# Reordering two short VectorE chains in a fused linear-attention and two-layer kernel

## The chip, the cores and the metric

The kernel runs on one core of one Trainium2 chip. The metric is device time in microseconds (us), as the median of several executions. Besides the time there is a trace of one execution per kernel, taken by the hardware profiler, with the start and length of each instruction on TensorE (PE, and PEld for its weight loads), VectorE (DVE), ScalarE (ACT), GpSimd (POOL) and the DMA queues.

## The reference

Eight batches of linear attention, then two dense layers on the result:

```python
q_p, k_p = phi(q), phi(k)                  # phi(x) = (x if x > 0 else exp(x) - 1) + 1
kv  = einsum('bhsd,bhse->bhde', k_p, v)
z   = sum(k_p, axis=2)
num = einsum('bhsd,bhde->bhse', q_p, kv)
den = einsum('bhsd,bhd->bhs', q_p, z)[..., None] + 1e-06
x   = (num / den) reshaped to [4608, 512]
h   = x @ w_in                             # 512 -> 2048
out = (h - tanh(h)) @ w_out                # 2048 -> 512
```

q, k and v are [8, 8, 576, 64]. Inputs and output are float32.

## The kernel before

The 4608 rows are worked in nine blocks of 512. A block has a first layer (16 tiles of four matmuls, `l1mm`), then a second layer in 16 "slots" of four matmuls (`l2mm`). The attention of the batch that the next block needs is put between these, as functions appended to a slot (`s2[n]`, run after the matmuls of slot n). The batch 0 attention comes first, in an opening that has no dense work to hide behind. In the code, `z` is the sum of k, `kv` the product of k and v, `zc` and `kz` their masked copies out of PSUM on VectorE, `den` the denominators, `split` the reciprocal cut into bf16 pieces (its last result is called w), and `spread` the matmuls that broadcast w to where the numerators stand.

The opening, where the first change acts:

```python
    b0_zc(0)            # VectorE: z of the first pairs out of PSUM
    b0_kv(0)            # TensorE: kv of the first pairs
    b0_kz(0)            # VectorE: kv of the first pairs out of PSUM
    b0_z(1)             # TensorE: z of the second pairs
    b0_zc(1)            # VectorE: z of the second pairs out of PSUM
    a_den(0, Banks([4]))   # TensorE: den; its second half needs zc(1). Then 1/den on VectorE
    ns0 = new_ns(0)
    b0_rest()
    b0_num(0, ns0)      # TensorE: num; needs kz(0)
    b0_kv(1)
    b0_kz(1)
    b0_spread((0, 2), 0)   # TensorE: needs 1/den
```

The second layer of the first block, where batch 1 is prepared (cut):

```python
            s2[3].append(lambda: a_qphi(1, 0))
            s2[4].append(lambda: (a_qphi(1, 1), load_q(2), load_k(2), load_v(2)))
            s2[0].append(prepare)
            s2[7].append(lambda: (a_qT_pe(1, 0, side), a_kv(1, side), a_qT_pe(1, 1, side)))
            s2[8].append(lambda: b0_scale_rest(side))
            s2[9].append(lambda: (a_den(1, side), num1(), a_split(1)))
            s2[11].append(lambda: spread1(0))
            # ... cut: exp2 = an exponential of batch 2 on ScalarE, rest2 = its VectorE part
            s2[11].append(lambda: (exp2(qs, q_t, qp_t, "qp", 0), rest2(qs[0])))
            s2[12].append(lambda: exp2(qs, q_t, qp_t, "qp", 1))
            s2[13].append(lambda: (spread1(1), exp2(ks, k_t, kp_t, "kp", 0), rest2(qs[1]), a_qT_dma(2)))
            s2[14].append(lambda: rest2(ks[0]))
```

The output copies of this block (`evac`, on ScalarE) come after slots 12 to 15.

## Time and profile before

| | before |
|---|---|
| median of 3 executions | 293.37 us (293.27 to 293.65) |
| span in the trace | 291.8 us |
| TensorE busy | 285.5 us, 98% |
| VectorE busy | 175.1 us, 60% |
| ScalarE busy | 139.7 us, 48% |

TensorE is full by this table, but its busy time counts modelled lengths: a dense 128x512 matmul is drawn 0.379 us long and the next one starts 0.216 us after it, so a wait of up to 0.16 us between two of them does not show in it, and a longer one shows only in part. Such a wait shows as a late start: one that comes later than 0.216 after the start before it, or than that plus 0.095 where the tile size changes.

### The profile page before, as it was taken

Reading aid. Unit: us, or ns where it says so; the run is one execution under the profiler, and the core shown is the slowest. Engines: PE = TensorE matmul, PEld = TensorE weight load, DVE = VectorE, ACT = ScalarE, POOL = GpSimd, SP = SyncE. Lnnn points to the kernel's source line nnn. Section 1 sums busy time; section 2 is a strip of 40 time slices with the busy share of each in tenths; the row PEclk is TensorE's granted clock in tenths of the full one; section 3 lists DMA queues with packets and bytes.
Section 4 is the critical chain, followed back from the end, with each engine's and each line's share of the span. In section 5 each row is a group of like instructions: output and inputs, shape, how many; then the busy total and the mean of one; then the engine's idle time right before and its main releaser. Section 6 shows DMA issues by size and latency. Waiting matters only on the chain.

```text
span 291.8 us, 4505 instructions
## 1 busy us (share of the span) xinstructions
PE 285.5 (98%) x1803; PEld 134.5 (46%) x1803; DVE 175.1 (60%) x266; ACT 139.7 (48%) x168; POOL 33.7 (12%) x56
## 2 busy tenths in 40 slices
PE   8999999999999999999999999999999999999994
PEld 3544464454454444444454444444544444444443
DVE  4759958987468674776478637865581457106600
ACT  4938548846354733465345534751551155126411
POOL 8674030110030003000300030000000000000000
PEclk9999999999999999999999999999999999999999
DMA  7999999997999768965895579666117310130032
GB/s 105 193 202 212 208 206 215 194 183 149 249 158 161 175 128 137 197 146 121 136 223 123 123 139 197 146 138 139 30 38 165 73 36 0 43 83 19 0 74 72
DMA packets 39093, 38.94 MB, mean 133 GB/s; under 512 B 16352, under 2 KB 33824, under 8 KB 38304
## 3 DMA queue, kind: packets, MB, share of 16 engines
q0 software_dynamic: 17568, 18.35, 39.0%
q1 hardware_dynamic: 21344, 20.17, 30.9%
q8 instruction: 14, 0.23, 0.3%
q10 hardware_dynamic: 160, 0.13, 0.1%
q14 instruction: 7, 0.06, 0.1%
HBM read 43.91 MB, written 9.55 MB: 183 GB/s over the span
## 4 chain that ended last, share of the span: by engine, by line
PE 85%; DMA 11%; POOL 2%; issue 1%; DVE 0%; POOLq 0%
PE ps_all L387 39%; PE ps_all L366 38%; DMA v<-in_v_dram 6%; DMA w_in_sb<-in_moe_w_in_dram 3%; PE ps_all L199 2%; DMA kraw<-in_k_dram 2%; PE ps_all L317 2%; PE ps_all L618 1%; PE ps_all L276 1%; POOL v L419 1%; PE ps_all L177 1%; POOL qraw L90 0%; PE ps_all L320 0%; POOL qraw L93 0%; POOL w_out_sb L115 0%
## 5 line engine op out<-in xcount | busy, mean ns | idle before, releaser
L366 PE MATMUL ps_all<-xT,w_in_sb 128*128 128x512 bf16 x574 | 127.6, 379 | 0.0
L387 PE MATMUL ps_all<-w_out_sb,gT 128*128 128x512 bf16 x560 | 127.5, 379 | 0.0
L373 DVE TENSOR_TENSOR gT<-ps_all,th 128x1024 bf16<-128x1024 f32 x64 | 77.9, 1218 | 59.2 <-ACT th L372 59.2
L372 ACT ACTIVATE th<-ps_all 128x1024 f32<-128x1024 f32 x64 | 65.6, 1025 | 57.1 <-PE ps_all L366 46.5
L366 PEld LDWEIGHTS <-w_in_sb 128*128 128x128 bf16 x574 | 55.0, 98 | 66.1 <-issue 0.3
L387 PEld LDWEIGHTS <-gT 128*128 128x128 bf16 x560 | 54.2, 98 | 64.2
L396 ACT COPY osb<-ps_all 128x512 f32<-128x512 f32 (+1 forms) x36 | 20.9, 583 | 71.8 <-PE ps_all L387 52.6
L328 DVE TENSOR_TENSOR xT<-ps_all,rdb 128x512 bf16<-128x512 f32 x24 | 16.5, 691 | 13.7 <-PE ps_all L317 11.2
L134 ACT ACTIVATE e<-qraw 128x1152 bf16<-128x1152 bf16 x16 | 18.5, 1160 | 8.2 <-DMA qraw<-in_q_dram 8.2
L134 ACT ACTIVATE e<-kraw 128x1152 bf16<-128x1152 bf16 x15 | 17.5, 1164 | 0.3 <-DMA kraw<-in_k_dram 0.3
L136 DVE TENSOR_TENSOR qp<-e,r 128x1152 bf16<-128x1152 bf16 x16 | 12.1, 758 | 8.0 <-ACT e L134 7.2
L136 DVE TENSOR_TENSOR kp<-e,r 128x1152 bf16<-128x1152 bf16 x15 | 11.4, 759 | 7.9 <-ACT e L134 6.9
L383 POOL COPY g<-qT 1x1 bf16<-1x1 bf16 x5 | 0.9, 178 | 119.2 <-DMA qT<-qp 119.2
L378 DVE TENSOR_TENSOR gT<-ps_all,th 128x512 bf16<-128x512 f32 x16 | 10.3, 686 | 2.4 <-ACT th L377 1.7
L377 ACT ACTIVATE th<-ps_all 128x512 f32<-128x512 f32 x16 | 9.2, 598 | 4.4 <-PE ps_all L366 3.2
L447 PE MATMUL ps_all<-zero 128*128 128x512 bf16 x29 | 9.2, 480 | 1.2 <-DVE zero L405 1.2
L317 PE MATMUL ps_all<-qT,kz 128*128 128x512 bf16 x28 | 10.1, 379 | 0.0
L135 DVE TENSOR_SCALAR r<-qraw 128x1152 bf16<-128x1152 bf16 x16 | 7.3, 454 | 2.1 <-DMA qraw<-in_q_dram 2.1
L199 PEld LDWEIGHTS <-kp 64*128 64x128 bf16 x216 | 6.4, 94 | 2.5 <-issue 2.1
L285 DVE RECIPROCAL rden<-den 128x144 f32<-128x144 f32 x7 | 7.4, 1053 | 0.2
L199 PE MATMUL ps_all<-vp,kp 64*128 64x136 bf16 x216 | 7.4, 220 | 0.0
L394 DVE COPY osb<-ps_all 128x128 f32<-128x128 f32 x1 | 0.3, 292 | 11.6 <-PE ps_all L618 11.6
(85 smaller groups left out, 123.6 us busy)
## 6 DMA issues: line engine op xcount, KB each, us to landing
out_dram<-osb SPq DMA_DIRECT2D x70, 128.0 KB
rdb<-ds SPq DMA_DIRECT2D x12, 576.0 KB
kraw<-in_k_dram POOLq DMA_DIRECT2D x7, 576.0 KB, 7.1
qraw<-in_q_dram POOLq DMA_DIRECT2D x7, 576.0 KB, 9.1
v<-in_v_dram POOLq DMA_DIRECT2D x7, 576.0 KB, 11.6
w_in_sb<-in_moe_w_in_dram POOLq DMA_DIRECT2D x6, 256.0 KB, 8.7
w_out_sb<-in_moe_w_out_dram POOLq DMA_DIRECT2D x3, 512.0 KB, 14.7
qraw<-in_q_dram POOLq DMA_DIRECT2D x2, 288.0 KB, 4.4
```

The lines of the kernel that those rows point to most:

```text
L134: return (lambda: nc.scalar.activation(e, x, AF.Exp), lambda: nc.vector.tensor_scalar(r, x, 0.0, 1.0, ALU.max, ALU.add), lambda: nc.vector ...
L136: lambda: nc.vector.tensor_tensor(y, e, r, ALU.min))
L199: nc.tensor.matmul(ps[hg][:, i, :], kp[r, i, j].rearrange("p h d -> p (h d)"), vp[r, i, j, :], start=(j == 0), stop=(j == J - 1))
L317: nc.tensor.matmul(ps, kz[:, p // 2, p % 2, 0:128], qT[:, p % 2, 0:8, p // 2, :], start=True, stop=True)
L328: nc.vector.tensor_mul(xT[:, p, S * b:S * b + 512].rearrange("p (j t c) -> p j t c", j=8, t=4), ps.rearrange("p j (t c) -> p j t c", t=4), ...
L366: nc.tensor.matmul(h, w_in_sb[:, 2 * (p % 2) + p // 2, fi * 128:(fi + 1) * 128], xT[:, p, c * 512:(c + 1) * 512], start=(n == 0), stop=(n ...
L372: nc.scalar.activation(th, h, AF.Tanh)
L373: nc.vector.tensor_sub(gT[:, fi:fi + 2, :], h, th)
L377: nc.scalar.activation(th, h, AF.Tanh)
L378: nc.vector.tensor_sub(gT[:, fi, :], h, th)
L387: nc.tensor.matmul(o, gT[:, fi, i * 128:(i + 1) * 128], w_out_sb[:, fi, :], start=(fi == 0), stop=(fi == NF - 1))
L396: nc.scalar.copy(osb[:, f0:f1], o[:, f0:f1])
```

## The change

The intent is to shorten two dependent chains. In the opening (the first part of the diff, below the "opening hunk"), den's second half waits for the z copy, which stands behind a kv copy on VectorE's queue; z is put first. In batch 1 (the "slot hunks"), den, num and split are run one slot sooner, and the two spreads with them.

```diff
     b0_zc(0)
     b0_kv(0)
-    b0_kz(0)
     b0_z(1)
     b0_zc(1)
+    b0_kz(0)
     a_den(0, Banks([4]))
...
-            s2[8].append(lambda: b0_scale_rest(side))
-            s2[9].append(lambda: (a_den(1, side), num1(), a_split(1)))
-            s2[11].append(lambda: spread1(0))
+            s2[8].append(lambda: (b0_scale_rest(side), a_den(1, side), num1(), a_split(1)))
+            s2[10].append(lambda: spread1(0))
...
-            s2[11].append(lambda: (exp2(qs, q_t, qp_t, "qp", 0), rest2(qs[0])))
-            s2[12].append(lambda: exp2(qs, q_t, qp_t, "qp", 1))
-            s2[13].append(lambda: (spread1(1), exp2(ks, k_t, kp_t, "kp", 0), rest2(qs[1]), a_qT_dma(2)))
+            s2[11].append(lambda: exp2(qs, q_t, qp_t, "qp", 0))
+            s2[12].append(lambda: (spread1(1), exp2(qs, q_t, qp_t, "qp", 1), rest2(qs[0])))
+            s2[13].append(lambda: (exp2(ks, k_t, kp_t, "kp", 0), rest2(qs[1]), a_qT_dma(2)))
```

## The prediction

> **What bounds the kernel now.** I read the page's busy shares first, then TensorE's own waits.
>
> ```profile
> PE 285.5 (98%) x1803; PEld 134.5 (46%) x1803; DVE 175.1 (60%) x266; ACT 139.7 (48%) x168; POOL 33.7 (12%) x56
> ```
>
> ```profile
> engine line waited for: us in total, times, longest us
> PE ps_all L447 <- DVE zero L405: 1.2, 1, 1.2
> PE ps_all L221 <- DMA v<-in_v_dram: 0.5, 1, 0.5
> PE ps_all L177 <- DMA v<-in_v_dram: 0.2, 1, 0.2
> PE ps_all L240 <- DVE xT L244: 0.2, 1, 0.2
> ```
>
> TensorE is the bound: busy for 98% of 291.8 us, with 2.1 us of listed waits, 1.2 of them before its first instruction. The change acts in two stages alone, the opening (to 18 us) and batch 1 (37 to 52 us), so I took the timeline there, by start times and not by lengths: a 128x512 matmul shows 379 ns but a new one starts every 216 ns, so a short wait hides inside the records. In the opening (VectorE and TensorE lines of the timeline, 8 to 20 us; start, length, engine, line):
>
> ```profile
> 12.37 0.40 PE L210 MATMUL ps_all<-one,kp 64*128 64x32 bf16 x18
> 12.59 0.43 DVE L225 TENSOR_TENSOR kz<-ps_all,mask 128x256 bf16<-128x256 f32 x1 [0.24 <-PE ps_all L221]
> 12.93 0.21 DVE L214 TENSOR_TENSOR kz<-ps_all,mask 128x64 bf16<-128x64 f32 x1
> 13.20 0.12 PEld L276 LDWEIGHTS <-kz 128*32 128x32 bf16 x8 [0.32 <-DVE kz L214]
> 13.44 0.61 PE L231 MATMUL ps_all<-qT,kz 128*128 128x512 bf16 x2
> 13.56 1.06 DVE L285 RECIPROCAL rden<-ps_all 128x144 f32<-128x144 f32 x1 [0.41 <-PE ps_all L276]
> 14.76 0.73 PE L240 MATMUL ps_all<-rden,sel 32*128 32x128 f32 x16
> ```
>
> The second half of the den matmuls (L276) stands 0.3 us behind the z copy (L214), which stands behind the kv copy (L225). That is the wait the first hunk aims at. Next I looked at what follows: two lines of the chain that ended last, then the timeline from 36 us.
>
> ```profile
> 22.32 16.50 DMA v<-in_v_dram
> 38.87 1.66 PE ps_all L177 x36
> ```
>
> ```profile
> 37.16 0.76 DVE L136 TENSOR_TENSOR qp<-e,r 128x1152 bf16<-128x1152 bf16 x1 [0.74 <-ACT e L134]
> 37.97 0.51 PEld L164 LDWEIGHTS <-qp 128*128 128x128 bf16 x9 [0.32 <-DVE qp L136]
> 38.87 1.43 PEld L177 LDWEIGHTS <-kp 64*128 64x128 bf16 x36 [0.40 <-DMA v<-in_v_dram]
> 45.77 0.37 DVE L298 SCALAR_TENSOR_TENSOR w<-t,part,u 128x144 bf16<-128x144 bf16 x1
> 46.20 0.30 PE L354 MATMUL ps_all<-w,sel 32*128 32x144 bf16 x8
> 47.34 1.16 ACT L134 ACTIVATE e<-qraw 128x1152 bf16<-128x1152 bf16 x1 [1.40 <-DMA qraw<-in_q_dram]
> 50.24 8.07 PE L366 MATMUL ps_all<-xT,w_in_sb 128*128 128x512 bf16 x36
> 51.47 1.07 ACT L396 COPY osb<-ps_all 128x512 f32<-128x512 f32 x2
> 52.10 5.71 PEld L366 LDWEIGHTS <-w_in_sb 128*128 128x128 bf16 x27 [0.26 <-issue]
> ```
>
> Three gates stand here, in order: v of batch 1 lands just before 38.87; the split reciprocal w ends at 46.14; the third output copy ends near 52.05 and the ninth matmul of the next block (PSUM bank 2) starts at 52.10. Before 38.87 the chain that ended last runs through DMA and GpSimd, not TensorE. After 52.10 TensorE starts its dense matmuls at an even 216 ns, apart from a switch of about 0.095 wherever it goes to smaller tiles (50.24 + 36 x 0.216 + the wait of 0.13 below = 58.15, and the next group, of 64-row tiles, starts at 58.24) or back.
>
> **What the Trainium skill says.** "Perfetto Trace Analysis", section "Tensor Engine Instruction (MATMUL, LD_WEIGHTS)", says a matmul's end is estimated from its size and not observed. The trace agrees: lengths of 379 ns at a pitch of 216; hence I count by starts. "PSUM — Partial Sum Buffer", section "Engine vs sequencer instructions", says ScalarE's and VectorE's queues are strictly first in, first out. The trace agrees: the z copy stood behind the kv copy although its matmuls' modelled end was 12.77 (12.37 + 0.40), and the output copies stand behind the exponentials. The same page, "PSUM bank collisions raise a hardware error", says to guard PSUM by bank and quadrant; here the bank-2 matmul starts at 52.10, 0.05 after the copy that empties that bank.
>
> **The change, part by part.** No instruction is added or removed; comparing the instruction orders, TensorE has four L387 matmuls moved from before the den group to behind the second spread, VectorE has z and kv swapped in the opening and the second pair of scalings moved ahead of the first q piece of batch 2; on ScalarE and the DMA queues the order is the same.
>
> Opening. Three latencies come from the lines: matmul end to copy start 0.04 (kv: end 12.55, copy 12.59), copy end to weight load 0.06 (13.14 to 13.20), and a VectorE successor starting 0.09 before its predecessor's end (12.93 against 13.02). With z first: z copy at 12.77 + 0.04 = 12.81 instead of 12.93, end 13.02, den resumes at 13.08 instead of 13.20: 0.12 sooner. The kv copy moves back: start 12.93, end 13.36. The num matmuls (L231) need it: 13.36 + 0.06 = 13.42 against 13.44, so TensorE gains only 0.02 there; den alone would have let them start at 13.32, and 0.10 of the 0.12 turns into a wait for kv. The reciprocal starts at 13.44 and ends at 14.50 instead of 14.62. If the spread (L240) waited for it, the gain is 0.12; if it waited for TensorE's own queue (its matmuls carry "issue" as cause), 0.02. So the opening is 0.02 to 0.12 us shorter up to the first dense matmul at 17.68.
>
> It does not get through. The transposes at 37.98 start right when qp is there (37.92 + 0.06), which hangs on a q load; and nine transposes take 0.52 us to the next start (40.46 to 40.98 for the later nine), so TensorE could start L177 at about 38.59 (37.98 + 0.52 + the switch of 0.095) and waits until 38.87 for v: 0.28 us. An earlier TensorE only waits longer. Net: 0.00.
>
> Batch 1. Before, den runs at 42.91 after the four matmuls of slot 9; after, at once behind the rest of batch 0: 4 x 0.216 = 0.865 sooner, 42.05. Its inputs are there (kz ends at 41.45, the last qT copy at 41.79). Bank reuse holds: num's third matmul needs the batch 0 rest product (ends 42.58) and comes at 42.75; the next needs den's copy (ends about 42.84) and comes at 42.97. So den, reciprocal and split all come 0.865 sooner, w at 45.27 instead of 46.14. But spread is moved by one slot as well. Between num and spread there are eight L387 matmuls before and eight after, so TensorE reaches the spread 0.865 sooner too: now 44.27 + 8 x 0.216 = 46.00, plus the 0.095 switch, 46.09, against w's 46.14 + 0.06. The real wait of 0.10 is kept, at 45.3. The second spread keeps its two slots behind the first as well. TensorE's work is the same, so the next block begins at 50.24 again. What really comes sooner is the last product for xT: the four scalings run together and end near 49.2 to 49.8 instead of 50.62. Its first reader is the fourth matmul of the block, at 50.24 + 3 x 0.216 = 50.89; 50.62 + 0.06 was in time already, so this buys slack of a microsecond and no time. Net: 0.00.
>
> Third gate. From 47.34 ScalarE runs without a gap: exp, copy, exp, copy, exp, copy, and starts when the q load lands. Its order is the same in both kernels. TensorE is ready for bank 2 at 50.24 + 8 x 0.216 = 51.97 and waits 0.13. Whatever batch 1 gained would be lost here too. Sum: 0.00 + 0.00, with the noise of where the loads land.
>
> **The rivals.** (1) The opening's gain gets through: 293.37 - 0.12 = 293.25. For: a TensorE at 98% passes on what it gains. Against: the v wait in the list. (2) The chain den to w is what counts, so all three gates fall: 0.28 + 0.10 + 0.13 = 0.51, 292.86. Against: the v and q loads do not start later or sooner with this change; over the first 60 us the software DMA queue took 98.6% of sixteen engines' time, so they land when the bytes are through. (3) Worse: VectorE now holds back the q pieces of batch 2 behind the second pair of scalings (the min of the first piece by about 1 us), and with it the transpose DMA of batch 2, the gate of the next loads at 56.88. Against: the last piece hangs on the exponential that ends at 50.03, and VectorE is then free; it should end near 51.6 instead of 51.85. If it did cost: 293.6 to 293.9.
>
> **Range and chances.** I take 293.3, with a little for the opening in runs where v lands sooner. Runs of before differ by 0.38 (293.27 to 293.65), by my reading where loads land, so 292.95 to 293.65. Two per cent is 5.9 us, more than ten times everything in rival 2: faster 0.005, slower 0.01, same 0.985.
>
> **What would show it.** Right: z's copy near 12.81, den's second half near 13.08, first dense matmul 0.02 to 0.12 sooner, L177 still starting with v near 38.9 and a longer wait; den near 42.05 with spread near 45.3 and the next block still near 50.24; bank 2 still after the third output copy. Wrong: L177 starting sooner by the opening's gain; a spread with no wait; the block starting sooner and bank 2 with it; or a new wait of TensorE after 58 us, which only a late transpose of batch 2 could cause.

## The result, and the profile after

The changed kernel took 293.44 us (median of 6 executions, 293.17 to 293.59). The kernel before, over six executions that include its first three, took 293.6 (293.27 to 293.74). The ratio is 0.9996 with a 95% interval of 0.9983 to 1.0009: the same. Ratios here are the mean time of one kernel's fast runs over that of the other's of the same rounds, so they are not quite the ratio of the medians quoted.

The page of the changed kernel, its first line of busy times, and the one of TensorE's listed waits that is new (us in total, times, longest):

```profile
PE 284.7 (98%) x1803; PEld 134.4 (46%) x1803; DVE 175.1 (60%) x266; ACT 139.8 (48%) x168; POOL 34.0 (12%) x56
```

```profile
PE ps_all L164 <- DVE qp L136: 0.9, 1, 0.9
```

The wait for v at L177 has left the list (it is still there, see below, but shorter and hidden by the modelled lengths), and a wait of 0.9 us for the first phi of batch 0's q has come in, at 7.6 us, in an opening that ran late in this execution. So the two traces can't be laid on each other by absolute time. Three lines of the kernel before that the prediction doesn't show (timeline; start, length, engine, line): the first kv matmul of the opening, the dense matmuls after it, and den of batch 1.

```profile
11.87 0.68 PE L221 MATMUL ps_all<-v,kp 64*128 64x128 bf16 x18 [0.47 <-DMA v<-in_v_dram]
...
17.68 2.55 PE L366 MATMUL ps_all<-xT,w_in_sb 128*128 128x512 bf16 x11
...
42.91 0.43 PE L276 MATMUL ps_all<-qT,kz 128*32 128x144 bf16 x16
```

The opening of the changed kernel:

```profile
12.15 0.68 PE L221 MATMUL ps_all<-v,kp 64*128 64x128 bf16 x18 [0.49 <-DMA v<-in_v_dram]
...
13.08 0.23 DVE L214 TENSOR_TENSOR kz<-ps_all,mask 128x64 bf16<-128x64 f32 x1 [0.43 <-PE ps_all L210]
13.22 0.41 DVE L225 TENSOR_TENSOR kz<-ps_all,mask 128x256 bf16<-128x256 f32 x1
13.36 0.12 PEld L276 LDWEIGHTS <-kz 128*32 128x32 bf16 x8 [0.20 <-DVE kz L214]
13.69 0.11 PEld L231 LDWEIGHTS <-kz 128*128 128x128 bf16 x2 [0.21 <-DVE kz L225]
...
13.72 1.06 DVE L285 RECIPROCAL rden<-ps_all 128x144 f32<-128x144 f32 x1
...
14.93 0.73 PE L240 MATMUL ps_all<-rden,sel 32*128 32x128 f32 x16
...
17.85 2.33 PE L366 MATMUL ps_all<-xT,w_in_sb 128*128 128x512 bf16 x10
```

The two VectorE copies have changed places. Counted from the first kv matmul (L221: 11.87 before, 12.15 here), den's second half comes at 1.21 instead of 1.33, the num weights now wait for the kv copy (cause "DVE kz L225", which was not there before), the reciprocal comes at 1.57 instead of 1.69, the spread (L240) at 2.78 instead of 2.89, and the first full dense matmul (L366) at 5.70 instead of 5.81. The stretch of batch 1 in the changed kernel:

```profile
37.99 0.64 PEld L164 LDWEIGHTS <-qp 128*128 128x128 bf16 x9 [0.18 <-DVE qp L136]
...
38.90 1.43 PEld L177 LDWEIGHTS <-kp 64*128 64x128 bf16 x36 [0.27 <-DMA v<-in_v_dram]
...
42.08 0.43 PE L276 MATMUL ps_all<-qT,kz 128*32 128x144 bf16 x16
...
44.94 0.37 DVE L298 SCALAR_TENSOR_TENSOR w<-t,part,u 128x144 bf16<-128x144 bf16 x1
45.37 0.12 PEld L354 LDWEIGHTS <-sel 32*128 32x128 bf16 x8 [0.53 <-DVE w L298]
...
46.85 1.17 ACT L134 ACTIVATE e<-qraw 128x1152 bf16<-128x1152 bf16 x1 [1.74 <-DMA qraw<-in_q_dram]
...
47.79 1.42 DVE L359 TENSOR_TENSOR xT<-ns,ps_all 128x576 bf16<-128x576 f32 x2 [0.58 <-PE ps_all L354]
...
50.27 7.93 PE L366 MATMUL ps_all<-xT,w_in_sb 128*128 128x512 bf16 x36
```

The weight load at L177 still waits for v. den is at 42.08 instead of 42.91 and w ends at 45.31 instead of 46.14, but the spread (L354) still stands behind w with the same 0.53. The next block begins at 50.27, against 50.24. Its 36 matmuls take 7.93 instead of 8.07: the wait for PSUM bank 2 (0.13) is gone, but q of batch 2 landed 0.49 us sooner in this execution (46.85 against 47.34), which I don't put down to the change: the load was issued no sooner (38.84 against 38.81), and in the slot hunks alone it landed at 47.39.

To compare executions whose opening starts at different times, I read distances between starts from each trace. They turn out constant to a few ns, except where a wait stands. The columns are: start of the first kv matmul of the opening; from there to the first dense matmul of 512 columns (L366); the wait for v of batch 1 (the distance from the first transpose of batch 1 to its first kv matmul, less the 0.598 that all traces without a wait show); from that kv matmul to the first matmul of the next block; the wait for bank 2 (ninth matmul of that block less the first, less 1.727).

| kernel | first kv | to dense | v wait | kv 1 to block | bank wait |
|---|---|---|---|---|---|
| before | 11.87 | 5.81 | 0.29 | 11.37 | 0.14 |
| before, second trace | 12.73 | 5.81 | 0 | 11.37 | 0 |
| after | 12.15 | 5.70 | 0.16 | 11.37 | 0 |
| after, second trace | 11.69 | 5.70 | 0.21 | 11.37 | 0.05 |
| opening hunk only | 11.92 | 5.70 | 0.16 | 11.37 | 0 |
| slot hunks only | 11.81 | 5.81 | 0.27 | 11.37 | 0.27 |
| den sooner, spread kept | 12.11 | 5.81 | 0.05 | 11.26 | 0 |
| before, no q load | 11.69 | 5.81 | 0 | 11.37 | 0 |
| after, no q load | 12.08 | 5.70 | 0 | 11.37 | 0 |
| no q load, den sooner | 12.01 | 5.70 | 0 | 11.26 | 0 |
| extra work before v | 12.24 | 5.81 | 0 | 11.37 | 0 |
| extra work after the gates | 12.09 | 5.81 | 0 | 11.37 | 0 |

From the first dense matmul to the first transpose of batch 1 it is 20.30 in every row (20.73 with the extra work before v), and from the ninth matmul of the next block on, nothing differs but the extra work. In the second traces of both kernels 28 of 1803 matmul records are missing, the first dense matmul's among them, which the gap of 0.43 between its neighbours shows (0.20 in the others); its start is set 0.226 ahead of the second one, as in the other traces.

One thing is not in the table: when v of batch 1 landed, by the semaphore of its load. In the nine traces with all loads (the two last versions left out) it was between 38.45 and 39.07 us, and where TensorE waited, the kv matmuls started some 0.046 after it. It is latest in the second trace of before, whose opening was the latest too, so the two are not independent. But TensorE doesn't set it: with the extra work before v it landed at 38.73, with that work after the gates at 38.75.

### The profile page after: what moved, and what is told of

It reads as the page before. It is cut to its first block, busy times and chain, and to the rows that moved or that the text cites. A ratio compares the mean times of both kernels' runs of the same rounds, so it can differ in the third digit from the quotient of the medians.

```text
span 291.6 us, 4505 instructions
## 1 busy us (share of the span) xinstructions
PE 284.7 (98%) x1803; PEld 134.4 (46%) x1803; DVE 175.1 (60%) x266; ACT 139.8 (48%) x168; POOL 34.0 (12%) x56
## 4 chain that ended last, share of the span: by engine, by line
PE 82%; DMA 13%; POOL 2%; ACT 1%; issue 1%; SPq 0%; DVE 0%; POOLq 0%
PE ps_all L366 38%; PE ps_all L387 37%; DMA v<-in_v_dram 6%; DMA w_in_sb<-in_moe_w_in_dram 3%; DMA kraw<-in_k_dram 2%; DMA out_dram<-osb 2%; PE ps_all L199 2%; PE ps_all L317 2%; PE ps_all L276 1%; POOL v L419 1%; ACT osb L396 1%; PE ps_all L177 1%; SPq L401 0%; POOL qraw L90 0%; PE ps_all L320 0%
## 5 line engine op out<-in xcount | busy, mean ns | idle before, releaser
L366 PE MATMUL ps_all<-xT,w_in_sb 128*128 128x512 bf16 x574 | 127.5, 379 | 0.0
L366 PEld LDWEIGHTS <-w_in_sb 128*128 128x128 bf16 x574 | 55.0, 98 | 66.0
L447 PE MATMUL ps_all<-zero 128*128 128x512 bf16 x29 | 8.2, 441 | 1.2 <-DVE zero L405 1.2
```

The source lines that it names most:

```text
L366: nc.tensor.matmul(h, w_in_sb[:, 2 * (p % 2) + p // 2, fi * 128:(fi + 1) * 128], xT[:, p, c * 512:(c + 1) * 512], start=(n == 0), stop=(n ...
```

## The experiments

Twelve kernels ran, each timed in five rounds against the kernel before. The first four shared a chip and runs of before, as did the next four and the last four. The kernel before scattered over about 0.6 to 1.1 us within one call (292.97 to 294.09 over all), so an interval of a ratio is about 0.0013, or 0.4 us, wide to each side. A tenth of a microsecond can be read from the traces' distances, and not from these times.

**The load of q taken out.** A gate is here a point where TensorE may have to wait for a load. To open these gates without a race, batch 1 is computed from batch 0's q, which stays in its buffer. The result is wrong for batch 1; it passed the comparison with the reference all the same, whose tolerance is too wide to see it.

```diff
-    load_q(1)
+    q_t[1] = q_t[0]
```

On the kernel before:

> The kernel before, with batch 1 computed from batch 0's q: the q load of batch 1 is gone (wrong result on purpose), and v of batch 1 and q of batch 2 should land several us sooner. My theory (v of batch 1 and q of batch 2 are gates for TensorE): the wait of 0.28 us before the kv matmuls of batch 1 and the wait of 0.13 us for PSUM bank 2 vanish, the wait of 0.10 us for w stays; 0.4 us shorter than before, near 293.0. Rival (TensorE is simply full and the waits for loads cost nothing that is not made up): same time as before within 0.1 us.

Measured: 293.06 us (before 293.43), ratio 0.9988 (0.9976 to 1.0001), which is 0.35 us less. Two lines of its timeline:

```profile
38.39 1.66 PE L177 MATMUL ps_all<-v,kp 64*128 64x192 bf16 x36
...
47.03 0.59 ACT L396 COPY osb<-ps_all 128x512 f32<-128x512 f32 x1 [0.52 <-PE ps_all L387]
```

The kv matmuls no longer show a wait for v, and the first output copy now waits for TensorE and not behind an exponential. Both load waits are 0 in the table, the wait for w stays. This is what the theory said, though the time alone does not exclude the rival.

On the changed kernel:

> The changed kernel with the same load taken out. My theory: with the gates of the loads open the opening's gain of 0.10 us gets through and nothing else does, since den and spread moved together; 0.10 us shorter than the kernel before without that load, about 0.5 us shorter than before; the wait for w stays at 0.10 us. Rival (the slot shift is worth its wait for w, 0.10 us, as well): 0.20 us shorter than the kernel before without the load, and no wait for w. Rival (the opening's gain is lost in the opening itself): equal to the kernel before without the load.

Measured: 293.24 us, ratio 0.9991 (0.9977 to 1.0004). Against the kernel before without the load the time is not shorter, as far as these intervals go. The trace shows 5.70 against 5.81 in the opening, no wait after it that could take this back, and 11.37 in batch 1. So by the distances the opening's 0.11 gets through with the gates open, and the slot hunks give nothing; the times (293.24 against 293.06) don't show the gain, and the 0.5 us against before came out as 0.26.

On the changed kernel with the spreads in their old slots (11 and 13):

```diff
-            s2[10].append(lambda: spread1(0))
+            s2[11].append(lambda: spread1(0))
-            s2[12].append(lambda: (spread1(1), exp2(qs, q_t, qp_t, "qp", 1), rest2(qs[0])))
-            s2[13].append(lambda: (exp2(ks, k_t, kp_t, "kp", 0), rest2(qs[1]), a_qT_dma(2)))
+            s2[12].append(lambda: (exp2(qs, q_t, qp_t, "qp", 1), rest2(qs[0])))
+            s2[13].append(lambda: (spread1(1), exp2(ks, k_t, kp_t, "kp", 0), rest2(qs[1]), a_qT_dma(2)))
```

> The changed kernel without that load, and with the spreads put back into their old slots, so that den alone is a slot sooner. My theory: twelve dense matmuls instead of eight lie between num and spread, w is there in time, the wait of 0.10 us goes; 0.10 us shorter than the changed kernel without the load, about 0.6 us shorter than before. Rival (the wait before the spread is a switch of tile sizes and not a wait for w): no difference between the two.

Measured: 292.94 us, ratio 0.9982 (0.997 to 0.9995), the shortest. Batch 1 takes 11.26 instead of 11.37. The wait for w was real, and what removes it is distance between num and spread, not an earlier slot.

**den sooner, spread kept, all loads as they are.** From the kernel before:

```diff
-            s2[8].append(lambda: b0_scale_rest(side))
-            s2[9].append(lambda: (a_den(1, side), num1(), a_split(1)))
+            s2[8].append(lambda: (b0_scale_rest(side), a_den(1, side), num1(), a_split(1)))
```

> The kernel before with den, num and split a slot sooner and the spreads left where they were; all loads as before. My theory: the wait of 0.10 us for w goes, but TensorE then waits as much longer for PSUM bank 2, whose copy stands on ScalarE behind exponentials that wait for q of batch 2: equal to before within 0.05 us, unless q lands sooner in a run. Rival (TensorE keeps what it gains): 0.10 us shorter, and the block of batch 1's columns starts 0.10 us sooner with the later matmuls following suit.

Measured: 293.58 us (before 293.43), ratio 1.0004 (0.9992 to 1.0017). Three lines of its timeline:

```profile
43.41 2.75 PE L387 MATMUL ps_all<-w_out_sb,gT 128*128 128x512 bf16 x12
...
44.91 0.37 DVE L298 SCALAR_TENSOR_TENSOR w<-t,part,u 128x144 bf16<-128x144 bf16 x1
...
46.09 0.30 PE L354 MATMUL ps_all<-w,sel 32*128 32x144 bf16 x8
```

Twelve dense matmuls lie between num and spread, w is ready at 45.28, and the spread starts when TensorE comes to it. The stretch is 0.106 shorter (11.261 against 11.367). In this execution q landed early (46.80), no bank wait stood, and so the rival was right for it: TensorE kept its gain. The time did not show it.

**The same extra work at two places.** Two matmuls of zeros, 0.43 us, in slot 1 of the first block's second layer, or in the first layer of the second block:

```diff
+                if c == 0 and s == 1:
+                    for _ in range(2):
+                        nc.tensor.matmul(ps_all[:, 1, :], zero[:, 0:128], zero, start=True, stop=True)
                 l2mm(gT, os_[i], i, 4 * g, 4 * g + 4)
```

```diff
             elif c != 2 or fi > 1:
+                if c == 1 and fi == 12:
+                    for _ in range(2):
+                        nc.tensor.matmul(h, zero[:, 0:128], zero, start=True, stop=True)
                 for p in range(NP):
                     l1mm(c, fi, h, p, p)
```

> The kernel before with two more 128x512 matmuls of zeros on TensorE (2 x 0.216 = 0.43 us) in the second layer of the first block, ahead of the gates. My theory: 0.28 us of it disappears in the wait for v of batch 1 and what is left, 0.15, largely in the wait of 0.13 us for PSUM bank 2: 0.0 to 0.15 us longer than before. Rival (TensorE is the bound all through): 0.43 us longer.

> The same two extra matmuls, but in the block after the gates (first layer of the second block, near 60 us). Both theories: 0.43 us longer than before, which shows that the size can be measured; mine also says that it is 0.3 to 0.4 us slower than the kernel with the same work ahead of the gates, the rival that the two are equal.

Measured: 293.92 us for the first, ratio 1.0018 (1.0005 to 1.0032), and 293.78 for the second, ratio 1.0013 (1.0001 to 1.0025), with before at 293.29. That is 0.53 and 0.38 us, each about the 0.43 that the rival says. My expectation for the first missed. Two lines of its timeline:

```profile
32.31 0.59 PE L629 MATMUL ps_all<-zero 128*128 128x512 bf16 x2
...
39.38 1.66 PE L177 MATMUL ps_all<-v,kp 64*128 64x192 bf16 x36
```

There is no wait for v left at 39.38, as I said. But this opening began 0.37 us later than in the first trace of before (12.24 against 11.87), and that alone would have used up the wait of 0.29. I had taken one execution's waits for the kernel's. The theory had to be amended: v lands when it lands, and TensorE waits only where it gets there sooner, which it does where its opening was early.

**Each half of the change alone.**

> The first hunk alone. My theory: the first dense matmul comes 0.10 us sooner counted from the first z matmul, TensorE waits 0.10 us longer for q or v of batch 1, time equal to before within 0.05 us. Rival (the gain gets through): 0.10 us shorter.

> The slot hunks alone. My theory: den, num, split and spread all 0.86 us sooner, the wait for w still 0.10 us, the next block begins as long after v's landing as before (about 11.4 us after the first kv matmul of batch 1); time equal to before within 0.05 us. Rival (a sooner den shortens the path): the block begins 0.10 us or more sooner after v.

Measured: the opening alone 293.24 us (before 293.29), ratio 0.9997 (0.9984 to 1.001); the slots alone 293.37, ratio 1.0 (0.9988 to 1.0013). The opening is 0.11 shorter in the first (5.70 against 5.81) and a v wait of 0.16 stands behind it, longer than the gain. In the second, batch 1 takes 11.372 us, against 11.367 before. Its trace also has the longest bank wait:

```profile
47.39 1.16 ACT L134 ACTIVATE e<-qraw 128x1152 bf16<-128x1152 bf16 x1 [2.40 <-DMA qraw<-in_q_dram]
...
50.16 8.20 PE L366 MATMUL ps_all<-xT,w_in_sb 128*128 128x512 bf16 x36
```

The q load landed at 47.39, and the 36 matmuls take 8.20 instead of 7.93. It belongs to that execution's load and not to the slots: in the changed kernel, which has the same slots, the wait was 0 and 0.05.

**Both kernels once more, unaltered.**

> The changed kernel once more, unaltered, because the runs so far show that the opening starts (first z matmul) between 10.9 and 11.4 us by when k of batch 0 lands, that v of batch 1 lands at 38.7 to 38.9 whatever TensorE does, and that q of batch 2 lands either near 46.8 or near 47.4. Theory as amended (the opening's gain is eaten only in runs whose opening was early): from the first dense matmul to the first transpose of batch 1 20.30 us, from there 0.60 us plus what is missing until v lands, 11.37 us to the next block, so the kv matmuls start at the later of v's landing and first dense matmul plus 20.90. Time as before within 0.1 us. Rival (the v wait belongs to the kernel and is always 0.2 to 0.3): kv starts 21.1 to 21.2 us after the first dense matmul.

> The kernel before once more, unaltered, for a second trace of the same code. Theory as amended: the first z matmul moves by up to 0.4 us against the first trace, the first dense matmul with it (6.6 to 6.7 us behind it), the wait for v shrinks by as much as the opening is later than in the first trace, and the wait for bank 2 is there only if q of batch 2 landed after 47.2. Rival (traces of one kernel repeat): first z at 11.0, v wait 0.28, bank-2 wait 0.13 again.

Measured: the changed kernel 293.35 us, ratio 0.9996 (0.9984 to 1.0009); the kernel before 293.37, ratio 0.9999 (0.9986 to 1.0013), with the shared runs of before at 293.43. Two lines of the second trace of before:

```profile
12.72 0.68 PE L221 MATMUL ps_all<-v,kp 64*128 64x128 bf16 x18 [0.25 <-DMA v<-in_v_dram]
...
39.43 1.66 PE L177 MATMUL ps_all<-v,kp 64*128 64x192 bf16 x36
```

The same code as in the first trace, but the first kv matmul is 0.86 us later and the first z matmul 1.08 (I expected up to 0.4), there is no wait for v (0.29 there) and none for bank 2 (0.14 there). The first dense matmul came 6.44 us after the first z matmul, not 6.6 to 6.7: that figure of mine missed. The first matmul after v is 0.56 later, not 0.86, so 0.3 of the lateness went into the wait. The amended theory held in kind, and the rival that traces of one kernel repeat fell. The amended theory's distances held for the changed kernel too: its kv matmuls came 21.10 us after the first dense matmul, 20.90 and a wait of 0.21 for v. The rival's 21.1 fits that trace as well; it falls by the traces with no wait. v itself landed at 38.45 and 39.07 in these two traces, outside the 38.7 to 38.9 that I had written.

**Two versions meant to beat both.** The first takes the whole batch 1 group a slot later so that v is there, keeps the spreads in their old slots, and moves one exponential behind the last output copy; the second also moves the spreads by half a slot. From the changed kernel, for the first:

```diff
-            s2[7].append(lambda: (a_qT_pe(1, 0, side), a_kv(1, side), a_qT_pe(1, 1, side)))
-            s2[8].append(lambda: (b0_scale_rest(side), a_den(1, side), num1(), a_split(1)))
-            s2[10].append(lambda: spread1(0))
+            s2[8].append(lambda: (a_qT_pe(1, 0, side), a_kv(1, side), a_qT_pe(1, 1, side)))
+            s2[9].append(lambda: (b0_scale_rest(side), a_den(1, side), num1(), a_split(1)))
+            s2[11].append(lambda: spread1(0))
...
-            s2[12].append(lambda: (spread1(1), exp2(qs, q_t, qp_t, "qp", 1), rest2(qs[0])))
-            s2[13].append(lambda: (exp2(ks, k_t, kp_t, "kp", 0), rest2(qs[1]), a_qT_dma(2)))
-            s2[14].append(lambda: rest2(ks[0]))
+            s2[12].append(lambda: (exp2(qs, q_t, qp_t, "qp", 1), rest2(qs[0])))
+            s2[13].append(lambda: (spread1(1), rest2(qs[1]), a_qT_dma(2)))
+            s2[15].append(lambda: (exp2(ks, k_t, kp_t, "kp", 0), rest2(ks[0])))
```

The second differs from the first in this (its VectorE part of the second q piece and the transpose go behind slot 14):

```diff
-            s2[11].append(lambda: spread1(0))
-            s2[13].append(lambda: (spread1(1), rest2(qs[1]), a_qT_dma(2)))
+            half = {12: lambda: spread1(0), 14: lambda: spread1(1)}   # run between matmuls 2 and 3 of the slot
+            s2[14].append(lambda: (rest2(qs[1]), a_qT_dma(2)))
```

> A version meant to beat both: the new opening; transposes and kv of batch 1 one slot later (so that v is there), rest, den and num behind slot 9, spreads in their old slots, and the exponential of k of batch 2 on ScalarE behind the last output copy of the block. Theory: no wait for v (0 to 0.29 before), none for bank 2 (0 to 0.27), the wait for w of 0.10 stays; from the first dense matmul to the ninth of the next block 33.99 us in every run, against 33.99 plus the two waits. 0.1 to 0.3 us shorter than before on average. Rival (the waits come back elsewhere, as a wait for bank 1 or for xT): no gain.

> The same, with the first spread two dense matmuls later still (in the middle of slot 12) and the second in the middle of slot 14, so that w is there as well. Theory: no wait left between the opening and the ninth matmul of the next block: 33.89 us from the first dense matmul, 0.2 to 0.4 us shorter than before on average. Rival (the second pair of scalings is too late for the next block, or a PSUM bank): a new wait of 0.1 us or more at the start of the next block, no gain over the other version.

Measured: 295.18 us, ratio 1.0054 (1.0041 to 1.0067), and 295.34 us, ratio 1.0072 (1.0052 to 1.0092). Both lost. One line of the first's timeline, and two of the second's:

```profile
40.41 1.25 PE L387 MATMUL ps_all<-w_out_sb,gT 128*128 128x512 bf16 x4 [2.09 <-DMA w_out_sb<-in_moe_w_out_dram]
```

```profile
39.97 1.02 PE L387 MATMUL ps_all<-w_out_sb,gT 128*128 128x512 bf16 x4 [1.93 <-DMA w_out_sb<-in_moe_w_out_dram]
...
51.21 1.41 DVE L359 TENSOR_TENSOR xT<-ns,ps_all 128x576 bf16<-128x576 f32 x2
```

The group in its old slot had covered another load: the matmuls of slot 8 need a piece of w_out that landed at 39.93 us in the second version, and at 40.09 in the kernel before, where slot 8 began at 40.98. With the group behind slot 8, TensorE comes to it some 2 us too soon. From the first dense matmul to the ninth of the next block the second version took 36.17 us, not the 33.89 expected. The first version's trace is of an execution of 297.15 us (the other six took 294.80 to 295.27): after its wait the granted clock was 0.5 from 41.07 to 44.49 us, and the kv matmuls took 2.57 us instead of 1.66. The wait stood before that; the other trace has it at full clock. Also, the second version's last scalings end at 52.62, and the fourth matmul of the next block, due 52.48, waits for them (it starts at 52.68), as the rival said. A version that keeps the group in slot 7, with den sooner, the spreads in slots 11 and 13 and the new opening, was run only without the q load; with the load it was not run.

## Why the prediction was right or wrong

The predicted time was 293.3 us, and 293.44 was measured, inside the stated range; "same" is what came out. The number proves little: rival 1's 293.25 lies in the range as well, and so would have passed. What can be judged are the steps, by the traces:

- **Opening.** Right, at the upper end of 0.02 to 0.12: it is 0.114 us shorter (5.697 against 5.811) in every trace with the new order. den's second half came 0.114 sooner (0.12 predicted) and num 0.02 sooner, where it turned into a wait for the kv copy, as worked out. The choice that the prediction left open is settled: the spread came 0.113 sooner, with the reciprocal, and not 0.02 sooner, with TensorE's queue.
- **"It does not get through ... Net: 0.00."** Right for the executions that can be judged but one, and too strong as a rule. In the three traces with the new opening and all loads, a v wait of 0.16 to 0.21 still stands, longer than the gain of 0.114, so the whole gain was lost there. In the five traces with the old opening, all loads and nothing put ahead of the gate, the wait was 0.29, 0.27, 0.05, 0 and 0. Where a wait stands already, v sets the start and a sooner TensorE only waits longer, so the first three would have let nothing through. In the other two TensorE came after v: the kv matmuls started 0.06 us after its landing in the kernel with extra work after the gates (38.80 against 38.75), and 0.36 after it in the second trace of before (39.43 against 39.07). Less the 0.046 from landing to start, that leaves room for 0.01 in the one and for the whole 0.11 in the other. My estimate from these eight traces is a mean gain of (0.01 + 0.11) / 8 = 0.015 us. The times can't confirm it, and no trace of the new opening with all loads shows a gain getting through.
- **The q gate at the transposes.** Wrong: it was a coincidence of that trace. From the first dense matmul to the first transpose it is 20.30 in all traces without extra work ahead of it, whether TensorE came early or late; q of batch 1 held it in none of them.
- **Batch 1.** Right: counted from the first kv matmul of batch 1, den came at 3.18 instead of 4.04, 0.86 sooner (0.865 predicted), the wait for w stayed, and the stretch is 11.37 before and after. The last scalings ended at 49.21 (49.2 to 49.8 predicted), slack that nothing used. The runs with spread kept show what the wait for w is worth: 0.106 us.
- **Third gate.** The mechanism is shown by two traces: with q at 47.34 and 47.39 TensorE waited 0.14 and 0.27 for bank 2. That whatever batch 1 gains would be lost there was too strong: one execution's wait was taken for the kernel's. With q at 46.7 to 47.0 the wait was 0 to 0.05, and with q at 47.43, where the extra work had made TensorE itself late, it was 0.
- **Rivals.** Rival 2 did not happen, because den and spread moved together. Rival 3 did not either: the last q piece of batch 2 ended at 51.68 (50.92 + 0.76; 51.6 predicted). Its load came sooner in that trace, but with the slot hunks alone and q at 47.39 it ended at 51.56, against 51.85 before. Rival 1 would hold in executions like the second trace of before; no run shows it with all loads.
- **Range.** That the scatter comes from where the loads land is supported by the two traces of before, 0.86 us apart in the opening: the later one's span is 0.37 us longer (292.17 against 291.80), near the 0.86 less the two waits of 0.29 and 0.14 that it doesn't have. But the range took three executions for the scatter; before ran from 292.97 to 294.09, wider than 292.95 to 293.65.

What stays open: whether the change is worth some 0.02 us or nothing, which intervals of 0.4 us cannot tell.

## What to carry to other kernels

Moving a producer and its consumer by the same amount moves the wait between them and does not shorten it; give the pair more distance. Before a gain is written off behind a load, read the gate in several traces: a wait for a load is a difference between two moving times, and one trace shows one draw of it. And work that seems to stand in the way of a load may be covering the next one, as the batch 1 group did for w_out.

## What the Trainium skill lacked or had wrong

- "TensorE: Matmul & The Clock Gate", section "Back-to-back issue gap", gives about 131 ns a matmul as the sustained rate of pairs of weight load and 512-column matmul, and 216 ns for one in isolation. Here a stream of such pairs runs at 216 ns each: in the kernel with den sooner and spread kept, 12 of them take 2.59 us (43.41 to 46.09, less 0.095 for the switch), with a weight load for each. The section "Step-by-step: what each phase is for" of the same page gives 216 ns as the back-to-back gap, which agrees; the 131 does not.
- "TensorEngine Tiling (Array Packing)", section "Key Properties", says that changing the tiling mode drains TensorE, and gives no size for it there. In the trace of before, a smaller tile's first start comes 0.309 to 0.312 us after the last 512-column matmul's where nothing is waited for, instead of 0.216: 0.093 to 0.096 us for the switch. On the way back to 128x128 tiles it is 0.152 to 0.175 us from the last small matmul's start, which holds that matmul too.
- No page that I read says how far the landing of a load moves between executions of the same code. The two traces of the kernel before put its first kv matmul at 11.87 and 12.73 us, and the first exponential of batch 2's q, which waits for its load, started between 46.71 and 47.43 us over the nine traces of kernels with all loads, the two last versions left out.
